# A three-round convolution and token-mixing kernel: when chunks enter their round, and where the weight loads and the adds of x are queued

## The chip, the cores and the metric

The kernel runs on one core of a Trainium2 chip. The metric is the device time of one execution in microseconds. TensorE (PE in the profile) multiplies and writes PSUM, VectorE (DVE) and ScalarE (ACT) read PSUM and work on SBUF, GpSimd (POOL) works on SBUF and issues DMAs that cast or accumulate, and SyncE (SP) issues plain DMAs.

## The reference

A short causal convolution feeds a token mixer and a channel mixer. Batch is 8, the sequence has 4224 tokens, the model width is 192.

```python
# weight: 8 heads x 7 taps, softmax over the taps; each head owns 24 channels
x = causal_conv(x, softmax(weight))          # out[s] = sum_k w[k] * x[s-6+k]
theta = x @ w_theta                          # 192 x 192
zr, zi = x * cos(theta), x * sin(theta)
y = einsum('ts,bsd->btd', w_tok_r, zr) + einsum('ts,bsd->btd', w_tok_i, zi)   # 4224 x 4224 each
u = x + y
out = u + maximum(u @ w_ch, 0)
```

The two products over tokens are nearly all of the work.

## The kernel before

**Chunks.** The tokens are cut into 33 chunks of 128. `Chunk` loads a chunk's input (`xw`, by POOL, with a halo of 16 rows that SP copies from the chunk before), and its `tasks` make the operands of the token product: `conv` (PE, evicted by ACT), `transpose` (PE; evicted by DVE for the first three chunks, by ACT afterwards), `theta` (PE, then two sines per half on ACT), `product` twice and `sums` twice (DVE). `conv` also stores the convolved x to the DRAM tensor `xs`. The second call of `sums` overwrites x, so it waits for that store.

**Units and steps.** The output tokens are cut into 17 units, 16 of them of two blocks of 128 tokens and one of a single block. A chunk must meet all 17 units. A step is one unit against all chunks that are resident; eleven chunks fit (`NW = 11`), so there are three rounds of eleven chunks. `start[k]` is the step at which chunk k enters; it stays for 17 steps. A chunk is prepared in the step before the one it enters at. There are 58 steps, and `n` is the number of chunks resident in a step. The steps from 41 on are final: they finish their unit and write the output. Of those, the steps with `n < 11` (53 to 57) are `late`.

**A step.** The complex product over two blocks is done with seven real products in place of eight (`runs`: seven runs of n chunks, two matmuls of 384 columns for each chunk). The operands of the weights are made by DVE in the step before (`w_tasks`: four transposes of 32x32 blocks, `turn`, and four sums, `wsum`), from two staging buffers `st` that POOL fills (`load_w`, four DMAs for the real weights, m = 1, and four for the imaginary ones, m = 2). There are two `st` buffers, so a load of step t+2 waits for step t+1's last transpose from the same buffer. After each run `give` adds the PSUM tile to the unit's rows `pv` on DVE; in the first round the four first writes are copies on ACT. The PSUM tiles of the runs have two buffers, so a run waits for the give of two runs before it. Rows of units that aren't finished go to DRAM (`part`) and come back 17 steps later.

**The order.** Each engine's instructions are chained by `in_order` in the order in which they are emitted. `step_events(t)` places the other work of a step by numbers from 0 to 7, the seven runs of the step. In the first steps there is no resident chunk to work on: there a loop over the eleven chunks emits the chunk's parts and, in `between`, lets the stream of the first steps advance by up to two (chunk, run) pairs at a time. `ready` holds the last chunk that is prepared, and the stream stops where it needs a later one. For the second and third chunk `between` also emits matmuls on zeros (`idle`).

**The adds of x.** u = x + y needs x once for each block. A block's x is added either by POOL in SBUF (`load_x` into `xr`, then `add_x`, which also waits for the last DVE instruction emitted before it), or in DRAM by an accumulating DMA from POOL (`add_ahead`) onto `part`. The DRAM adds are for the late steps. Each has a step of its own: 27, 29 and 31 for blocks whose x is known by then, 41 for the others.

**The end.** `outputs` finishes the final steps: cast of u to 16 bits, a transpose (by a DMA through the crossbar, `crossed`, where a step isn't late; by PE where it is), the product with `w_ch`, and `output` on DVE with the store. In the last two steps the cast of the first half of the channels is DVE's.

Of the kernel before, what the change touches and what calls it, by code (L numbers as in the profile page):

```python
# [9 lines left out]
AT = mybir.ActivationFunctionType  # L10
ALU = mybir.AluOpType
F16 = mybir.dt.float16
# [4 lines left out]
def kernel(  # L17
# [23 lines left out]
    nc = tc.nc  # L41
# [3 lines left out]
    P = nc.NUM_PARTITIONS  # L45
    assert (B, D, P) == (8, 192, 128) and S % P == 0
    N = B * D
# [4 lines left out]
    NK = S // P  # L52
# [7 lines left out]
    NU = (NT + 1) // 2  # L60
    NW = 11
    PC = 512

    base = [0, 0, 1, 1, 2, 3, 3, 4, 4, 5, 5]
    assert len(base) == NW
# [7 lines left out]
    SYNC = mybir.DependencyInfo(  # L73
        mybir.DependencyClass.Sync, mybir.DependencyReason.SCHED_ONLY
    )
    last = {}

# [31 lines left out]
    xs = dram.tile([S, N], F16, name="xs")  # L109
    part = [dram.tile([NT, P, N], F32, name=f"part{i}") for i in range(2)]  # L110
# [36 lines left out]
    def evacuate(out, in_, by_dve=False):  # L147
        if by_dve:
            dve(nc.vector.tensor_copy(out=out, in_=in_))
        else:  # L150
            act(nc.scalar.activation(out=out, in_=in_, func=AT.Copy))  # L151
# [133 lines left out]
    class Step:  # L285


        def __init__(self, t):
            self.t, self.u, self.ks = t, unit(t), active(t)
            self.n = len(self.ks)  # L290
            self.tbs = [tb for tb in (2 * self.u, 2 * self.u + 1) if tb < NT]
            self.pair = len(self.tbs) == 2
            self.first = t < NU
            self.final = t + NU >= NSTEP
            self.late = self.final and self.n < NW
            visits = [v for v in range(NU, NSTEP) if v % NU == t % NU]
            quiet = [v for v in visits if start[2 * NW - 1] < v <= 2 * NU]
            self.adds, self.ahead = [], []
            for i, tb in enumerate(self.tbs):
                known = self.known(tb)  # L300
                if t not in ([v for v in quiet if known < v - 1] or visits[-1:])[:1]:
                    continue
                if not self.late:
                    self.adds.append(i)
                else:
                    far = known <= start[2 * NW - 1]
                    self.ahead.append((i, 2 * NU - NW + 2 * (t % NU) if far else start[-1],
                                       (t // NU - 1 - far) % 2))
            self.time = 0.324 * self.n * (7 if self.pair else 4)
            self.st, self.w, self.xr, self.ub, self.uT, self.pv = {}, {}, {}, {}, {}, []  # L310

        def known(self, tb):

# [60 lines left out]
                    )  # L374
                self.pv.append(pv)

        def load_x(self, i):
            self.xr[i] = wk.tile([P, N], F16, name="xr", tag="xr", bufs=1)
            nc.sync.dma_start(
                out=self.xr[i], in_=xs[self.tbs[i] * P : (self.tbs[i] + 1) * P, :]  # L380
            )
# [9 lines left out]
        def add_ahead(self, i, which):  # L391

            tb = self.tbs[i]
# [113 lines left out]
    steps = [Step(t) for t in range(NSTEP)]  # L507
# [5 lines left out]
    def step_events(t):  # L513
        found = []
        s = steps[t]
        if t + 1 < NSTEP:
            found += steps[t + 1].w_tasks()
            found.append((1.6, steps[t + 1].load_rows))
            for i in steps[t + 1].adds:
                found.append((2 + 2 * i, lambda i=i: steps[t + 1].load_x(i)))  # L520
                found.append((3.6 + 2 * i, lambda i=i: steps[t + 1].add_x(i)))
        here = [(r, i, which) for r in steps for i, when, which in r.ahead if when == t]
        for j, (r, i, which) in enumerate(here):
            found.append((1.5 + 1.8 * j, lambda r=r, i=i, which=which: r.add_ahead(i, which)))
        if t + 2 < NSTEP:
            nxt = steps[t + 2]
            for m in (1, 2):
                found.append((1.3 + 3 * (m - 1), lambda m=m: nxt.load_w(m)))
        for at, f in outputs:
            begin = at - sum(s.time for s in steps[:t])  # L530
            if 0 <= begin < steps[t].time:
                found.append((7 * begin / steps[t].time, f))
        if t >= NU - 2:
            new = [k for k in range(NK) if start[k] == t + 2 and k >= NW]
            for k in new:
                found.append((4.5, lambda k=k: load_chunk(k)))
            at = 0.1
            for k in (k for k in range(NK) if start[k] == t + 1 and k >= NW):
                pos = [0, .5, 1.4, 2.2, 2.6, 3.1, 3.15, 3.4, 3.6]

                def add(at, j, k):
                    def go():
                        if j == 0:
                            chunks[k].todo = chunks[k].tasks()
                        next(chunks[k].todo)()
                    found.append((at, go))
                for j, p in enumerate(pos):
                    add(at + p, j, k)
                at += 2.3
        return found  # L550
# [29 lines left out]
    def idle(n):  # L580
# [17 lines left out]
        out=wsum, in_=wsb, axis=mybir.AxisListType.X, op=ALU.add  # L598
# [5 lines left out]
        out=wdiag, in0=wsb[0:KS, :, :],  # L604
        in1=ident[0:KS, 0:KS].unsqueeze(1).to_broadcast([KS, H, KS]), op=ALU.mult,
# [130 lines left out]
```

## Time and profile before

| | |
|---|---|
| median of 3 runs | 1450.12 us (1448.14 to 1450.21) |
| the profiled execution's own time | 1448.14 us |
| its span, first to last instruction | 1446.4 us |
| PE busy | 1416.3 us, 98% of the span |
| DVE busy | 979.2 us, 68% |
| POOL busy | 435.1 us, 30% |
| ACT busy | 315.5 us, 22% |
| y matmuls (`mix`, L443) | 7656, busy 1283.6 us |
| gives on DVE (L408) | 324, mean 954 ns |
| weight transposes on DVE (L336) | 224, mean 1465 ns |
| adds of x on POOL (L386) | 24, mean 3105 ns |

The profile's lines give a line of the kernel, an engine, an operation, the tiles written and read, a count, the busy time and the mean duration, and the idle time of the engine before these instructions with what ended it. A line of the windows gives a stretch of time, its length, the busy time of PE, of its weight loads (PEld), of DVE, ACT and POOL, each with a count of instructions, the granted TensorE clock as a share of full speed, the mean share of busy DMA engines, and GB/s. A line of the waits gives who waited for whom: microseconds in total, how often, the longest. A line of the timeline gives the start, the duration, the engine, the line, the operation with its tiles and the count of instructions merged.

### The profile page before, as it was taken

The page shows a single profiled execution, that of the slowest core. Times are in us where ns is not written, and L with a number is a line of the kernel's source. Part 1 is how long each engine was busy: PE and PEld are TensorE (multiplying, and loading weights), DVE is VectorE, ACT ScalarE, POOL GpSimd, SP SyncE. Part 2 cuts the span into 40 slices and gives each one's busy share as a digit, 9 for nine tenths or more (in the row PEclk, how much of TensorE's full clock was granted, in tenths as well). Part 3 has the DMA queues.
Part 4 walks back from the last instruction along what each step waited for, and adds up shares of the span by engine and source line. Part 5 has one row for each costly group of instructions (what it writes and reads, how often), then busy time and mean ns, then how long its engine had stood idle before and what let it go on. Part 6 is the DMA issues. An engine that isn't in the chain of part 4 may idle for free.

```text
span 1446.4 us, 23748 instructions
## 1 busy us (share of the span) xinstructions
PE 1416.3 (98%) x9809; PEld 887.9 (61%) x9809; DVE 979.2 (68%) x1051; ACT 315.5 (22%) x379; POOL 435.1 (30%) x655
## 2 busy tenths in 40 slices
PE   7899999999999999999999999999999999999997
PEld 5556666666666666666666666666666666666665
DVE  6893555545548777866666657877777667767686
ACT  5861101111134254000000004435210110010133
POOL 7431211111233232432433342233323123213120
PEclk9999999999999999999999999999999999999999
DMA  9986756465699998998899989999999999998893
GB/s 173 227 178 145 146 103 149 90 149 97 137 231 219 214 250 217 228 254 183 213 256 213 242 143 245 228 188 234 279 216 206 209 204 221 204 203 194 166 222 125
DMA packets 272029, 281.99 MB, mean 195 GB/s; under 512 B 106672, under 2 KB 240176, under 8 KB 271920
## 3 DMA queue, kind: packets, MB, share of 16 engines
q0 software_dynamic: 162464, 92.15, 48.4%
q1 hardware_dynamic: 71824, 178.88, 35.1%
q10 hardware_dynamic: 37632, 9.44, 4.1%
q8 instruction: 77, 1.26, 0.3%
q14 instruction: 32, 0.26, 0.1%
HBM read 245.49 MB, written 108.13 MB: 244 GB/s over the span
## 4 chain that ended last, share of the span: by engine, by line
PE 89%; DVE 4%; DMA 3%; POOL 2%; ACT 1%; issue 1%; SPq 0%; DVEq 0%; ACTq 0%; POOLq 0%
PE y L443 82%; PE v L141 5%; PE pc L210 1%; PE tp L165 1%; POOL st L323 1%; DMA xw<-in_x_dram 1%; DVE z L257 1%; DVE wt L336 1%; DVE pv L408 1%; ACT z L246 1%; DVE z L251 0%; DVE pv L476 0%; DVE wt L348 0%; POOL xw L197 0%; DMA xs<-z 0%
## 5 line engine op out<-in xcount | busy, mean ns | idle before, releaser
L443 PE MATMUL y<-z,wt 128*128 128x384 f16 x7656 | 1283.6, 326 | 10.6 <-DVE pv L408 7.5
L443 PEld LDWEIGHTS <-wt 128*128 128x128 f16 x7656 | 740.8, 98 | 488.6 <-issue 10.6
L408 DVE TENSOR_TENSOR pv<-y,pv 128x768 f32<-128x768 f32 x324 | 308.9, 954 | 323.6 <-PE y L443 282.8
L336 DVE STREAM_TRANSPOSE wt<-st 128x1408 f16<-128x1408 f16 (+7 forms) x224 | 327.8, 1465 | 48.5 <-PE y L443 39.0
L323 POOL DMA_DIRECT2D st<-in_moe_w_tok_r_dram x232 | 132.5, 578 | 466.1 <-DVE wt L336 461.0
L323 POOL DMA_DIRECT2D st<-in_moe_w_tok_i_dram x232 | 132.7, 578 | 404.4 <-DVE wt L336 388.9
L348 DVE TENSOR_TENSOR wt<-wt 128x1408 f16<-128x1408 f16 (+7 forms) x216 | 176.7, 818 | 40.8 <-PE y L443 38.4
L151 ACT ACTIVATE z<-pc 128x768 f16<-128x768 f32 x65 | 53.2, 819 | 387.2 <-PE pc L210 386.9
L151 ACT ACTIVATE ub<-pv 128x768 f16<-128x768 f32 x63 | 50.2, 835 | 333.0 <-DVE pv L408 310.4
L406 ACT ACTIVATE pv<-y 128x768 f32<-128x768 f32 x66 | 54.0, 819 | 282.0 <-PE y L443 282.0
L141 PEld LDWEIGHTS <-uT 128*128 128x128 f16 x1056 | 91.0, 98 | 25.8 <-issue 7.9
L386 POOL TENSOR_TENSOR pv<-pv,xr 128x1536 f32<-128x1536 f32 x24 | 74.5, 3105 | 68.6 <-DVE pv L476 22.1
L197 POOL DMA_DIRECT2D xw<-in_x_dram x132 | 76.4, 585 | 31.0 <-DMA xw<-xw 8.7
L476 DVE SCALAR_TENSOR_TENSOR pv<-v,pv 128x768 f32<-128x768 f32 x66 | 62.9, 954 | 27.5 <-PE v L141 27.1
L257 DVE TENSOR_TENSOR z<-z 128x768 f16<-128x768 f16 x132 | 73.4, 556 | 3.6
L151 ACT ACTIVATE uT<-tp 128x1536 f16<-128x1536 f16 (+1 forms) x48 | 58.2, 1215 | 74.4 <-PE tp L165 74.4
L246 ACT ACTIVATE z<-v,half_pi 128x768 f16<-128x768 f32 x66 | 59.8, 907 | 41.2 <-PE v L141 40.8
L251 DVE TENSOR_TENSOR z<-z 128x1536 f16<-128x1536 f16 x66 | 60.0, 947 | 7.5 <-ACT z L246 7.5
L141 PE MATMUL v<-wth,uT 128*128 128x192 f16 x528 | 55.0, 248 | 4.4 <-ACT z L246 3.0
L141 PE MATMUL v<-wch,uT 128*128 128x192 f16 x528 | 54.2, 246 | 2.1 <-DVE pv L476 1.2
L246 ACT ACTIVATE z<-v 128x768 f16<-128x768 f32 x66 | 53.4, 809 | 0.0
L210 PE MATMUL pc<-xw,bands 96*64 96x192 f16 x528 | 35.8, 258 | 2.6 <-ACT bands L625 1.1
(44 smaller groups left out, 142.4 us busy)
## 6 DMA issues: line engine op xcount, KB each, us to landing
part<-pv SPq DMA_DIRECT2D x79, 768.0 KB, 4.3
pv<-part SPq DMA_DIRECT2D x79, 768.0 KB, 6.1
out_dram<-pv SPq DMA_DIRECT2D x66, 384.0 KB, 4.3
st<-in_moe_w_tok_r_dram POOLq DMA_DIRECT2D x136, 176.0 KB, 5.5
st<-in_moe_w_tok_i_dram POOLq DMA_DIRECT2D x136, 176.0 KB, 5.1
xs<-z SPq DMA_DIRECT2D x132, 96.0 KB, 4.5
xw<-in_x_dram POOLq DMA_DIRECT2D x121, 96.0 KB, 6.1
xr<-xs SPq DMA_DIRECT2D x24, 384.0 KB, 3.7
```

What stands on the lines that cost most here:

```text
L141: pe(nc.tensor.matmul(v[:, k, b * D : (b + 1) * D], lhsT=tT[:, 3 * k + b + i, :], rhs=w[:, 2 * b + i, :], start=(i == 0), stop=(i == 1),))
L151: act(nc.scalar.activation(out=out, in_=in_, func=AT.Copy))
L197: nc.gpsimd.dma_start(out=self.xw[lo : lo + n, h, :, :], in_=x[:, t0 : t0 + n, :].rearrange("b s d -> s b d"),)
L246: act(nc.scalar.activation(**args))
L257: dve(nc.vector.tensor_tensor(out=z[:, o, :], in0=z[:, a, :], in1=z[:, b, :], op=ALU.subtract))
L323: pool(nc.gpsimd.dma_start(out=st[a * Q : (a + 1) * Q, 0:nb, :, 0:n] .rearrange("i r bt s -> i (r bt) s"), in_=w[self.tbs[0] * P : (self.t ...
L336: dve(nc.vector.transpose(self.w[name][:, 0 : self.n, :, :], self.st[int(name[1])][:, int(name[0]) - 1, :, 0 : self.n * Q] .rearrange("p b ...
L348: dve(nc.vector.tensor_tensor(out=self.w[name][:, 0 : self.n, :, :], in0=self.w[a][:, 0 : self.n, :, :], in1=self.w[b][:, 0 : self.n, :, : ...
L386: ins = pool(nc.gpsimd.tensor_tensor(out=self.pv[i], in0=self.pv[i], in1=self.xr[i], op=ALU.add))
L408: dve(nc.vector.tensor_tensor(out=o, in0=yv, in1=o, op=ALU.add))
L443: pe(nc.tensor.matmul(y[cn][:, q, 0:BH], lhsT=self.w[wn][:, c, :, :].rearrange("p bt i -> p (bt i)"), rhs=chunks[k].z[:, zn, q * BH : (q + ...
L476: dve(nc.vector.scalar_tensor_tensor(out=ub, in0=channel_mix(self.uT[i][:, 6 * g : 6 * g + 6, :], wch), scalar=0.0, in1=ub, op0=ALU.max, o ...
```

## The change

- **Entry.** The three rounds get lists of their own. The first round's chunks enter at steps 0, 0, 0, 1, 1, 2, 2, 3, 3, 4, 4 in place of 0, 0, 1, 1, 2, 3, 3, 4, 4, 5, 5. The second round's enter two at a time at steps 18 to 22 and one at 23. The third round's list is as before. The number of chunks in steps 0 to 5 is 3, 5, 7, 9, 11, 11 in place of 2, 4, 5, 7, 9, 11; in steps 17 to 22 it is 8, 8, 8, 8, 8, 10 in place of 9, 9, 10, 9, 9, 9; in steps 35 to 40 it is 9, 9, 9, 8, 8, 9 in place of 9, 9, 10, 9, 9, 9. There are 58 steps as before.
- **Start-up.** x of chunk 2 is loaded ahead of the weights of step 0, and x of chunk 3 ahead of the weights of step 1. DVE's weight work of step 0 is emitted after the sums of chunk 0, not after the theta of chunk 0.
- **Adds of x.** On POOL: x is loaded at the add, at 3.3 and 5.0 of the step, and the add doesn't wait for DVE any more. In DRAM: the adds of a late step come four steps ahead of it, in steps 49 to 53.
- **Casts.** All casts are ACT's.

```diff
-    base = [0, 0, 1, 1, 2, 3, 3, 4, 4, 5, 5]
-    start = [base[k % NW] + (NU + 1) * (k // NW) for k in range(NK)]
+    base = [[0, 0, 0, 1, 1, 2, 2, 3, 3, 4, 4],
+            [0, 0, 1, 1, 2, 2, 3, 3, 4, 4, 5],
+            [0, 0, 1, 1, 2, 3, 3, 4, 4, 5, 5]]
+    start = [base[k // NW][k % NW] + (NU + 1) * (k // NW) for k in range(NK)]
...
+            self.ahead = self.late or 0 <= t + NU - NSTEP < 2
...
-        def load_x(self, i):
-            self.xr[i] = wk.tile([P, N], F16, name="xr", tag="xr", bufs=1)
-            nc.sync.dma_start(
-                out=self.xr[i], in_=xs[self.tbs[i] * P : (self.tbs[i] + 1) * P, :]
-            )
...
-            ins = pool(nc.gpsimd.tensor_tensor(
-                out=self.pv[i], in0=self.pv[i], in1=self.xr[i], op=ALU.add
-            ))
-            tc.add_manual_dep(ins.ins, last["dve"].ins.name, SYNC, reason="pace")
...
+            rows = slice(self.tbs[i] * P, (self.tbs[i] + 1) * P)
+            if not self.ahead:
+                xr = wk.tile([P, N], F16, name="xr", tag="xr", bufs=1)
+                nc.sync.dma_start(out=xr, in_=xs[rows, :])
+                pool(nc.gpsimd.tensor_tensor(
+                    out=self.pv[i], in0=self.pv[i], in1=xr, op=ALU.add
+                ))
+                return
             for cols in (slice(0, HN), slice(HN, N)):
                 pool(nc.gpsimd.dma_start(
-                    out=part[which][tb, :, cols], in_=xs[tb * P : (tb + 1) * P, cols],
-                    accum_op=ALU.add,
+                    out=part[(self.t // NU - 1) % 2][self.tbs[i], :, cols],
+                    in_=xs[rows, cols], accum_op=ALU.add,
                 ))
...
-            evacuate(self.ub[i][:, cols], self.pv[i][:, cols], self.t >= NSTEP - 2 and g == 0)
+            act(nc.scalar.activation(
+                out=self.ub[i][:, cols], in_=self.pv[i][:, cols], func=AT.Copy
+            ))
...
-            for i in steps[t + 1].adds:
-                found.append((2 + 2 * i, lambda i=i: steps[t + 1].load_x(i)))
-                found.append((3.6 + 2 * i, lambda i=i: steps[t + 1].add_x(i)))
+            if not steps[t + 1].ahead:
+                for i in steps[t + 1].adds:
+                    found.append((3.3 + 1.7 * i, lambda i=i: steps[t + 1].add_x(i)))
+        for s in steps[t:]:
+            if s.ahead and t == s.t - (4 if s.late else 10):
+                for i in s.adds:
+                    found.append((3.3 + 1.7 * i, lambda s=s, i=i: s.add_x(i)))
...
     steps[0].load_rows()
+    load_chunk(2)
     for m in (1, 2):
         steps[0].load_w(m)
-    load_chunk(2)
+    load_chunk(3)
     for m in (1, 2):
         steps[1].load_w(m)
...
-        if i == 1:
-            for _, f in steps[0].w_tasks():
-                f()
         if i + 3 < NW:
             load_chunk(i + 3)
...
         if old:
             old.sums(1)
+        if i == 1:
+            for _, f in steps[0].w_tasks():
+                f()
         between(1)
```

More of the change, by code (lines that the diff above doesn't have):

```diff
@@ L62 @@
     PC = 512
-    base = [0, 0, 1, 1, 2, 3, 3, 4, 4, 5, 5]
-    assert len(base) == NW
-    start = [base[k % NW] + (NU + 1) * (k // NW) for k in range(NK)]
+    base = [[0, 0, 0, 1, 1, 2, 2, 3, 3, 4, 4],
+            [0, 0, 1, 1, 2, 2, 3, 3, 4, 4, 5],
+            [0, 0, 1, 1, 2, 3, 3, 4, 4, 5, 5]]
+    assert all(len(b) == NW for b in base)
+    start = [base[k // NW][k % NW] + (NU + 1) * (k // NW) for k in range(NK)]
     NSTEP = start[-1] + NU
@@ L71 @@
         mybir.DependencyClass.NoSync, mybir.DependencyReason.DATA
-    )
-    SYNC = mybir.DependencyInfo(
-        mybir.DependencyClass.Sync, mybir.DependencyReason.SCHED_ONLY
     )
@@ L295, in __init__ @@
             self.late = self.final and self.n < NW
+            self.ahead = self.late or 0 <= t + NU - NSTEP < 2
             visits = [v for v in range(NU, NSTEP) if v % NU == t % NU]
-            quiet = [v for v in visits if start[2 * NW - 1] < v <= 2 * NU]
-            self.adds, self.ahead = [], []
+            self.adds = []
             for i, tb in enumerate(self.tbs):
[L300 to L303, printed above, removed]
+                at = [v for v in visits if self.known(tb) < v - 1 and v + NU < NSTEP
+                      and start[2 * NW - 1] < v <= 2 * NU]
+                at = at[0] if at else visits[-1]
+                if t == at:
                     self.adds.append(i)
[L305 to L308, printed above, removed]
             self.time = 0.324 * self.n * (7 if self.pair else 4)
-            self.st, self.w, self.xr, self.ub, self.uT, self.pv = {}, {}, {}, {}, {}, []
+            self.st, self.w, self.ub, self.uT, self.pv = {}, {}, {}, {}, []
         def known(self, tb):
@@ L375, in load_rows @@
                 self.pv.append(pv)
-        def load_x(self, i):
-            self.xr[i] = wk.tile([P, N], F16, name="xr", tag="xr", bufs=1)
-            nc.sync.dma_start(
-                out=self.xr[i], in_=xs[self.tbs[i] * P : (self.tbs[i] + 1) * P, :]
-            )
-        def add_x(self, i):
-            ins = pool(nc.gpsimd.tensor_tensor(
-                out=self.pv[i], in0=self.pv[i], in1=self.xr[i], op=ALU.add
-            ))
-            tc.add_manual_dep(ins.ins, last["dve"].ins.name, SYNC, reason="pace")
-        def add_ahead(self, i, which):
-            tb = self.tbs[i]
+        def add_x(self, i):
+            rows = slice(self.tbs[i] * P, (self.tbs[i] + 1) * P)
[6 more added lines that the diff above has]
+                return
             for cols in (slice(0, HN), slice(HN, N)):
                 pool(nc.gpsimd.dma_start(
-                    out=part[which][tb, :, cols], in_=xs[tb * P : (tb + 1) * P, cols],
-                    accum_op=ALU.add,
+                    out=part[(self.t // NU - 1) % 2][self.tbs[i], :, cols],
+                    in_=xs[rows, cols], accum_op=ALU.add,
                 ))
@@ L518, in step_events @@
             found.append((1.6, steps[t + 1].load_rows))
-            for i in steps[t + 1].adds:
-                found.append((2 + 2 * i, lambda i=i: steps[t + 1].load_x(i)))
-                found.append((3.6 + 2 * i, lambda i=i: steps[t + 1].add_x(i)))
-        here = [(r, i, which) for r in steps for i, when, which in r.ahead if when == t]
-        for j, (r, i, which) in enumerate(here):
-            found.append((1.5 + 1.8 * j, lambda r=r, i=i, which=which: r.add_ahead(i, which)))
+            if not steps[t + 1].ahead:
[5 more added lines that the diff above has]
+                    found.append((3.3 + 1.7 * i, lambda s=s, i=i: s.add_x(i)))
         if t + 2 < NSTEP:
```

## The prediction

> **What bounds the kernel now.** The page comes first: is one engine full all the way?
>
> ```profile
> span 1446.4 us, 23748 instructions
> ...
> PE 1416.3 (98%) x9809; PEld 887.9 (61%) x9809; DVE 979.2 (68%) x1051; ACT 315.5 (22%) x379; POOL 435.1 (30%) x655
> ...
> L443 PE MATMUL y<-z,wt 128*128 128x384 f16 x7656 | 1283.6, 326 | 10.6 <-DVE pv L408 7.5
> ```
>
> PE is the bound and idles 30 us. The count of y matmuls doesn't change (each of 33 chunks meets every unit once), nor does the number of steps (58). So only PE's idle time can change, and the waits of PE, with the windows, say where it lies (PE busy, PEld, DVE, ACT, POOL in each):
>
> ```profile
> PE y L443 <- DVE pv L408: 5.1, 5, 2.5
> PE y L443 <- ACT pv L406: 3.0, 3, 1.2
> ...
> PE pc L210 <- DMA xw<-in_x_dram: 0.9, 1, 0.9
> ```
>
> ```profile
> 90.00:100.00 10.00, 10.00 (x71) 6.55 (x70) 9.76 (x15) 6.24 (x9) 2.34 (x4) 1.00 0.84 241
> 100.00:110.00 10.00, 7.54 (x48) 4.33 (x46) 9.79 (x12) 0.63 (x1) 3.40 (x6) 1.00 0.59 78
> ...
> 140.00:440.00 300.00, 300.00 (x1898) 181.73 (x1896) 155.33 (x140) 46.18 (x56) 61.92 (x108) 1.00 0.66 136
> ```
>
> These waits are those of the first 110 us. From 110 to 1340 us PE waits 2.9 us in all, and 3.6 us at the end. The start-up alone has slack, and it ends when DVE, full from 90 us on, gives PE a PSUM buffer back: the last wait, 2.46 us, ends at 104.61. DVE's timeline shows how the start-up is ordered:
>
> ```profile
> 24.68 0.70 DVE L336 STREAM_TRANSPOSE wt<-st 128x512 f16<-128x512 f16 x1
> 25.59 0.96 DVE L149 COPY uT<-tp 128x1536 f16<-128x1536 f16 x1 [0.20 <-PE tp L165]
> ...
> 46.24 1.15 DVE L257 TENSOR_TENSOR z<-z 128x768 f16<-128x768 f16 x2
> ```
>
> The first weight transpose of step 1 comes just ahead of the copy that releases chunk 2's theta matmuls. Today its weights landed long ago; the reader should keep this pair in mind.
>
> **Start-up.** Three edits meet: step 0 takes three chunks, step 0's weight work moves behind chunk 0's sums, and x of chunks 2 and 3 is issued ahead of weights. What they remove: the 0.9 us wait for chunk 3's x, and some waits at runs of two chunks, which last 0.65 us against 0.8 to 0.95 us for one eviction.
> What they add, in order. DVE ran step 0's weight work at 15.35 to 18.1, in a gap waiting for PE; now the gap stays empty and the work starts when chunk 0's sums end, at 24.77. Four transposes and four sums at three chunks lie between the rows at two (0.43, 0.29) and four (0.70, 0.42): 4 x 0.57 + 4 x 0.36 = 3.7, so to 28.5. Step 1's first weight buffer is free after the second transpose, 25.9; POOL issues four loads by 28.5 (4 x 0.57); they land between 2.4 and 5 us later, 3.5 taken: 32.0. DVE waits for them, 3.5 us. Then the transpose (0.84) and the copy of chunk 2: 33.8, against 26.55 today. PE stands from about 27.1 to 33.8, since its queue is in order. Behind those loads on POOL stand x of chunks 4 and 5 (issued 30.8 to 35.4, landing 4.9 later, so 38 for chunk 4, whose matmuls come at about 39: covered by 1 us, 2 us lost if they are late). On SP chunk 2's copies between buffers now come ahead of chunk 0's stores of x (14.48 today, about 15.5 then), which chunk 0's last two sums await at 23.5; at 4.6 to land, 3 us of cover stay. Step 0's own weights are issued 2.3 later, behind x of chunk 2, and aren't used before 24.77.
> Part of the delay is absorbed: today PE loses 3.1 us at 33 to 39 to evictions of step 0, which come later now. DVE: chunk 1 products and sums (1.82 + 2.34) to 37.95, chunk 2 to 42.1, a transpose to 43.0; chunk 3's sine I put at 44.6 (45.0 today), then product 0.91, sum 0.48, transpose 0.84, product 0.91: chunk 3's sums start at 47.8, today at 46.24.
> From there to the give that frees PE, DVE's queue as built holds: seven chunks at 4.16 and chunk 3's sums 2.34, 31.5; eight gives at 0.95, 7.6; transposes 0.84 + 4 x 1.10 + 4 x 1.37, 10.7; weight sums 3 x 0.48 + 4 x 0.63 + 3 x 0.79, 6.3. Together 56.1. Today the same list is 54.9 in 58.4 us (46.24 to 104.61), so 3.5 idle. Half of that idle: 47.8 + 56.1 + 1.6 = 105.5.
> At its stall PE has done 224 y matmuls today and 196 then, 28 fewer, each 0.1625 us (1938 in 315.1 us): 4.55 us more left. 105.5 + 4.55 - 104.6 = **+5.4**. Loads landing at 30.9 and no idle give +2.8; 33.5, all the idle and late x give +9.
>
> *The clock.* In the windows of 2 us the granted clock is 0.72 at 38:40, 0.50 at 40:42, 0.93 at 42:44, after PE's gaps at 33 to 39. I let one such dip move to 34 us and count nothing.
> The Trainium skill ("TensorE: Matmul & The Clock Gate", Part 1) says that an idle window of about 3.4 us halves the clock and about as long a busy one restores it, which speaks against a PE gap of 6.7 us. If its dip came in addition to today's, the sum would be 2 us more by an estimate from that page.
>
> **Later rounds.** Steps 17 to 21 now have eight chunks and two new ones each. DVE per step: seven gives 6.7, four transposes (between 1.10 and 1.37) 4.9, four sums 2.8, two chunks 8.3: 22.7. PE: 8 x 14 x 0.1625 = 18.2, and two chunks at 3.5 (0.52 x 2 + 0.83 + 0.82 x 2): 25.2. That is 90%, against 23.5 of 27.5 in today's two-chunk steps at nine (85%), where waits of 0.3 to 0.7 us appear. Five such steps in a row, a little each: +0.8 (-0.5, if fewer single collisions fall badly, to +4, if each step loses one eviction, 0.95).
>
> **Adds of x on POOL** lose their wait on a DVE instruction, and x is loaded at the add. POOL may wait a landing more (3.7) ahead of a weight load. Today DVE waits 8.1 us for weights, and PE for none of it: DVE waits 283 us for PE, which is the cover. 0 (-0.5 to +1). Without cover an add costs its 3.1.
>
> **Late adds in DRAM.** 18 accumulating DMAs that ran at 678 to 1046 us now run in steps 49 to 53, beside the crossbar transposes, two ahead of each weight load of POOL. Each takes 0.86 to issue and 9.1 to land. A load issued at 4.3 of 7 of a step is used at 2.2 of the next: 4.9/7 of 25 us, 17 us, against 1.7 + 9.1 + 5.9. Little is left over, so +0.3 (0 to +3); their absence from 678 to 1046 frees nothing that PE waits for.
>
> **Last casts.** Three casts of 0.55 on DVE become 0.83 on ACT. ACT's last part is on the path: a 0.83 cast started at 1434.05 delays the copy at 1434.66 by 0.2, and the first is 0.28 longer: +0.5 (0 to 1.3).
>
> Sum: 5.4 + 0.8 + 0 + 0.3 + 0.5 = +7.0. The profiled execution took 1448.14 (span 1446.4 and 1.7 around it), 2.0 below the median of 1450.12. 1446.4 + 7.0 + 1.7 = 1455.1, and 1457 against the median.
>
> **Rivals.** *Faster:* the start-up follows PE's and ACT's cadence, not DVE's queue. Then the last theta matmul (93.2 today) comes 1.3 earlier for eight y matmuls fewer ahead of it, and up to 4.6 (PE's idle time from 40 to 93, evictions above all) earlier still: 87.3 to 91.9; the give follows 7.6 later as today, 94.9 to 99.5. With 4.55 for the 28 matmuls that is -5.2 to -0.6, about -3: 1447. For it speak the 8.1 us of eviction waits; against it DVE's 98% in the same place. It decides only if chunk 3's sums start before 104.6 - 4.55 - 56.1 = 43.9.
> *No change:* DVE's idle time today (3.5, and 3.5 at the wait for loads) hides it all: within 2.9 us, 1450.
> *More than start-up:* the two-chunk steps lose an eviction each (+4), and the late adds hold one weight load past its use (+3): 5.4 + 4 + 3 + 0.5 = +13, 1463. For it: DMA share about 1.0 in those stages. Against it: PE full in all of them now.
>
> **Numbers.** A measurement can tell 0.2%, 2.9 us. Forecast, +3 to +10: 0.62; the third rival: 0.13; no change 0.12; faster 0.13. Slower is 0.75. The range runs from 1449, most of no change, to 1463, the third rival's sum.
>
> **What would show it.** A DVE wait for the r weights of step 1 at about 28 us; chunk 2's copy at 33 to 35; a PE gap there with the clock falling; PE's last start-up wait ending at 103 to 108 with 196 y matmuls done; PE waits of under 0.7 in steps 17 to 21; the last casts on ACT. It is wrong if that last wait ends before 100, or if PE loses more than 4 us after 110.

## The result, and the profile after

The changed kernel takes 1484.92 us (median of 4 runs, 1478.22 to 1490.04), the kernel before, measured beside it, 1449.13. The ratio is 1.0246, interval 1.0203 to 1.029: slower by about 36 us where +7 was forecast and 1463 was the upper end. The sign was right, and the size was wrong by a factor of five.

The profiled execution of the changed kernel is its slowest, 1490.04 us with a span of 1488.2. From its page, the span, the engines and the y matmuls:

```profile
span 1488.2 us, 23738 instructions
...
PE 1426.6 (96%) x9809; PEld 890.9 (60%) x9809; DVE 1016.4 (68%) x1048; ACT 318.1 (21%) x382; POOL 435.9 (29%) x655
...
L431 PE MATMUL y<-z,wt 128*128 128x384 f16 x7656 | 1289.1, 327 | 17.1 <-DVE pv L396 12.9
```

The work of PE is the same, 9809 matmuls. The span is 41.8 us longer: PE stands idle for 61.6 us in place of 30.1 (31.5 more), and is busy for 10.3 us more on the same matmuls; the granted clock is lower after its gaps (0.91 over the first 112 us in place of 0.98, 0.94 from 1340 us to the end of the run). DVE, with fewer instructions, is busy for 37 us more. The waits of PE name the places (total, how often, the longest):

```profile
PE v L140 <- DMA uT<-ub: 13.7, 3, 7.5
PE y L431 <- DVE pv L396: 12.9, 16, 2.8
PE pc L209 <- ACT z L150: 6.0, 1, 6.0
PE v L140 <- DVE uT L148: 5.0, 2, 4.8
...
PE y L431 <- DVE wt L331: 2.5, 1, 2.5
```

Of these five, only the second is in the profile before (7.5, 10, 2.5). The windows put them in time (columns as in the table of before: PE, PEld, DVE, ACT, POOL, then clock, DMA share and GB/s):

```profile
90.00:100.00 10.00, 9.84 (x90) 6.77 (x89) 7.67 (x10) 9.14 (x12) 2.34 (x4) 0.96 0.39 67
100.00:110.00 10.00, 8.52 (x59) 5.17 (x57) 9.69 (x14) 4.35 (x6) 0.00 (x0) 1.00 0.37 70
110.00:120.00 10.00, 7.55 (x47) 4.57 (x47) 8.02 (x10) 1.62 (x2) 5.69 (x10) 1.00 0.90 189
140.00:440.00 300.00, 300.00 (x1848) 180.64 (x1847) 146.28 (x128) 38.94 (x48) 59.56 (x104) 1.00 0.61 124
440.00:600.00 160.00, 155.89 (x1226) 99.09 (x1224) 122.58 (x153) 68.72 (x78) 49.38 (x87) 1.00 1.00 232
1340.00:1400.00 60.00, 53.75 (x343) 33.51 (x341) 34.93 (x39) 6.31 (x8) 21.51 (x29) 0.94 1.25 189
```

Before, PE lost 2.9 us in all between 110 and 1340. Now it loses 4.1 us between 440 and 600 alone, where the kernel before has

```profile
440.00:600.00 160.00, 159.27 (x1206) 100.93 (x1204) 126.47 (x148) 57.43 (x66) 52.59 (x86) 1.00 0.99 230
```

It loses 2.4 us between 600 and 870, where it lost nothing before, and 6.2 between 1340 and 1400. So the start is not the only stage that loses time.

DVE's timeline shows the pair that the prediction pointed at, the weight transpose of step 1 ahead of chunk 2's copy:

```profile
26.42 0.36 DVE L343 TENSOR_TENSOR wt<-wt 128x384 f16<-128x384 f16 x1
30.48 0.85 DVE L331 STREAM_TRANSPOSE wt<-st 128x640 f16<-128x640 f16 x1 [3.69 <-DMA st<-in_moe_w_tok_r_dram]
31.24 0.92 DVE L148 COPY uT<-tp 128x1536 f16<-128x1536 f16 x1
```

The wait is there, 3.69 us (3.5 was worked out), and the copy is 5.65 us later than before. But 50 us later comes a wait that no sentence of the prediction mentions. ACT's timeline and then PE's:

```profile
84.73 0.81 ACT L150 ACTIVATE z<-pc 128x768 f16<-128x768 f32 x1 [7.71 <-DMA part<-pv]
```

```profile
85.59 0.85 PE L209 MATMUL pc<-xw,bands 96*64 96x192 f16 x8 [5.96 <-ACT z L150]
...
112.45 5.85 PE L431 MATMUL y<-z,wt 128*128 128x384 f16 x35 [2.78 <-DVE pv L396]
```

ACT wants to write chunk 9's z tile and waits until a store to `part` has landed: the tile takes a buffer of the z pool that a row of step 1 still occupies (`z_free` below tests this). SP issues that store at 78.55 us, and it lands 6.08 us later:

```profile
78.55 0.34 SPq L444 DMA_DIRECT2D part<-pv  x1
```

In the kernel before, step 1's two rows go out about 8 us earlier. They land after 3.4 and 4.8 us, by 75.6, one to three microseconds ahead of the first copy into chunk 9's z tile:

```profile
70.14 1.02 SPq L456 DMA_DIRECT2D part<-pv  x2
```

```profile
76.74 0.93 ACT L151 ACTIVATE z<-pc 128x768 f16<-128x768 f32 x1
```

PE, which waits for ACT, stands for 6 us, DVE runs dry (7.15 us), and the last wait of the start ends at 112.45, not at 105.5. At that moment 196 y matmuls have been done, as predicted.

### The profile page after: what moved, and what is told of

It is laid out like the page before. It is cut to its first block, busy times and chain, and to the rows that moved or that the text cites. A ratio compares the mean times of both kernels' runs of the same rounds, so it can differ in the third digit from the quotient of the medians.

```text
span 1488.2 us, 23738 instructions
## 1 busy us (share of the span) xinstructions
PE 1426.6 (96%) x9809; PEld 890.9 (60%) x9809; DVE 1016.4 (68%) x1048; ACT 318.1 (21%) x382; POOL 435.9 (29%) x655
## 4 chain that ended last, share of the span: by engine, by line
PE 76%; DVE 11%; DMA 7%; ACT 2%; issue 2%; SPq 1%; POOL 0%; ACTq 0%; DVEq 0%
PE y L431 70%; PE v L140 4%; DMA uT<-ub 3%; DVE pv L396 2%; DVE wt L343 2%; DVE z L250 2%; DVE z L256 2%; DVE wt L331 2%; ACT z L245 1%; PE tp L164 1%; PE pc L209 1%; DMA xw<-xw 1%; DMA st<-in_moe_w_tok_r_dram 1%; DMA part<-pv 1%; DMA xs<-z 1%
## 5 line engine op out<-in xcount | busy, mean ns | idle before, releaser
L431 PE MATMUL y<-z,wt 128*128 128x384 f16 x7656 | 1289.1, 327 | 17.1 <-DVE pv L396 12.9
L431 PEld LDWEIGHTS <-wt 128*128 128x128 f16 x7656 | 742.4, 98 | 498.7 <-issue 22.6
L331 DVE STREAM_TRANSPOSE wt<-st 128x1408 f16<-128x1408 f16 (+8 forms) x224 | 327.5, 1465 | 46.9 <-PE y L431 41.5
L343 DVE TENSOR_TENSOR wt<-wt 128x1408 f16<-128x1408 f16 (+8 forms) x216 | 217.0, 1005 | 46.8 <-PE y L431 44.6
L378 POOL TENSOR_TENSOR pv<-pv,xr 128x1536 f32<-128x1536 f32 x24 | 74.9, 3120 | 15.1 <-DMA xr<-xs 11.1
L140 PE MATMUL v<-wch,uT 128*128 128x192 f16 x528 | 55.5, 249 | 15.6 <-DMA uT<-ub 13.7
```

Source lines behind the costliest of these rows:

```text
L140: pe(nc.tensor.matmul(v[:, k, b * D : (b + 1) * D], lhsT=tT[:, 3 * k + b + i, :], rhs=w[:, 2 * b + i, :], start=(i == 0), stop=(i == 1),))
L331: dve(nc.vector.transpose(self.w[name][:, 0 : self.n, :, :], self.st[int(name[1])][:, int(name[0]) - 1, :, 0 : self.n * Q] .rearrange("p b ...
L343: dve(nc.vector.tensor_tensor(out=self.w[name][:, 0 : self.n, :, :], in0=self.w[a][:, 0 : self.n, :, :], in1=self.w[b][:, 0 : self.n, :, : ...
L378: pool(nc.gpsimd.tensor_tensor(out=self.pv[i], in0=self.pv[i], in1=xr, op=ALU.add))
L431: pe(nc.tensor.matmul(y[cn][:, q, 0:BH], lhsT=self.w[wn][:, c, :, :].rearrange("p bt i -> p (bt i)"), rhs=chunks[k].z[:, zn, q * BH : (q + ...
```

## The experiments

The change consists of four edits that can be made one by one: the start (entry lists, order of the first loads, place of step 0's weight work), the POOL adds, the late DRAM adds, and the casts. My first theory after the trace was a sum over places: start 12, two-chunk steps and POOL adds 7.7, the end 22.

### The edits alone

`late_alone`, the late DRAM adds alone:

```
-  self.ahead.append((i, 2 * NU - NW + 2 * (t % NU) if far else start[-1],
-                     (t // NU - 1 - far) % 2))
+  self.ahead.append((i, t - 4, (t // NU - 1) % 2))
...
-  found.append((1.5 + 1.8 * j, ... add_ahead(i, which)))
+  found.append((3.3 + 1.7 * j, ... add_ahead(i, which)))
```

> The kernel before with one edit alone: the 18 accumulating DMAs of the last nine blocks are issued four steps ahead of their step (steps 49 to 53) and no longer in steps 27 to 41. Theory (they hold the crossbar transposes back): uT<-ub lands in 10 to 27 us instead of 5 to 9, PE waits 10 to 15 us for uT behind those transposes between 1330 and 1410, two or three halvings of the granted clock follow, and the time is 17 to 25 us above before. Rival 1 (the transposes suffer only because the other edits shift the end's timing or put all casts on ACT): 0 to +5. Rival 2, the prediction's own reading (a weight load is held a little): +0.3, at most +3.

Measured: 1449.03, ratio 1.0001 (0.9991 to 1.001). No cost at all; the theory fell, as did my reading of the end as an effect of this edit by itself. The transposes do land later (median 9.1 us of those after 1200, longest 10.9, in place of 6.9 and 8.3), but nobody waits.

`start_alone`, the three edits of the start:

> The kernel before with the new entry lists, the new order of the first loads and step 0's weight work behind chunk 0's sums; adds and casts as before. Theory: the start-up costs 12 us (10 us of PE idle time and about 2 of halved clock, the wait of 6 for a z tile that a row of step 1 still holds among them) and the two-chunk steps 3 to 5: +15 to +17. Rival (the prediction's sum: start-up 5.4, later rounds 0.8, the wait for the z tile being an accident of that run): +6. Rival 2 (the start-up's loss is made good later): under +4.

Measured: 1471.56, ratio 1.0163 (1.0147 to 1.0179), +22.6. This is the largest part by far. The wait for the z tile is there again (6.0), so it is no accident of one run, and the last stall ends at 113.34.

`pool_alone`, the POOL adds alone:

```
-  found.append((2 + 2 * i, ... load_x(i)))
-  found.append((3.6 + 2 * i, ... add_x(i)))
+  found.append((3.3 + 1.7 * i, ... load_x(i)))
+  found.append((3.3 + 1.7 * i, ... add_x(i)))
...
-  tc.add_manual_dep(ins.ins, last["dve"].ins.name, SYNC, reason="pace")
```

> The kernel before with the 24 adds of x on POOL changed alone: x loaded at the add, no wait on a DVE instruction. Theory: the adds now lie beside weight sums of DVE, which hold each other up: weight sums of the steps with adds take up to 4 us, DVE is busy 25 to 40 us more in all, PE waits 2 to 4 us more between 600 and 870 and about as much after 1050 none: +2 to +4. Rival (the prediction): DVE's waits for PE cover it, 0 (-0.5 to +1). What it leaves to see is whether the DVE growth comes with this edit alone.

Measured: 1451.40, ratio 1.002 (1.0011 to 1.003), +2.4. The group of DVE's weight sums, from the page of before and from this run's:

```profile
L348 DVE TENSOR_TENSOR wt<-wt 128x1408 f16<-128x1408 f16 (+7 forms) x216 | 176.7, 818 | 40.8 <-PE y L443 38.4
...
L348 DVE TENSOR_TENSOR wt<-wt 128x1408 f16<-128x1408 f16 (+7 forms) x216 | 211.2, 978 | 40.7 <-PE y L442 38.2
```

One of these sums on DVE's timeline, and what POOL does at that time:

```profile
703.07 4.49 DVE L348 TENSOR_TENSOR wt<-wt 128x1408 f16<-128x1408 f16 x1
```

```profile
703.69 3.12 POOL L386 TENSOR_TENSOR pv<-pv,xr 128x1536 f32<-128x1536 f32 x1
```

A sum of this shape takes 0.88 us with POOL idle. Beside the add it takes 4.49, and the add takes its usual 3.12. PE then waits for DVE's give (1.5 us between 600 and 870, nothing before). In the profile before, one add between 600 and 1340 us runs beside a weight sum (3.42 us at 612.70); in this run more than half of them do. The removed wait let an add begin only after a DVE instruction, but the edit also moves the adds, from 3.6 and 5.6 of the step, behind the sums emitted at 3.05, 3.3 and 5.1, to 3.3 and 5.0. Which of the two brings adds and sums together isn't shown.

`after_adds_back`, the changed kernel with only the late DRAM adds put back into steps 27 to 41:

> The changed kernel with the accumulating DMAs of the last nine blocks put back into steps 27 to 41. Theory: the end of the run recovers, PE waits for uT<-ub vanish, 17 to 25 us below the changed kernel, so +14 to +22 against before. Rival (the end's loss comes from the shifted start or from the casts on ACT): within 5 us of the changed kernel, +30 to +36.

Measured: 1473.82, ratio to before 1.0179 (1.016 to 1.0197), 11.1 below the changed kernel. Between the two theories. The sum of the start and the POOL adds alone is 25.0 and this kernel is 24.9 above before, so the casts on ACT, the one other edit in it, are worth nothing that these runs can tell (each interval reaches about 2.5 us to either side, and 0.5 was forecast). The late DRAM adds are worth 0 alone and 11 in company.

### Which company

`late_pool` and `late_start` join the late DRAM adds to one other edit each.

> The kernel before with two edits: the late accumulating DMAs (alone: 1.0001 of before) and the POOL adds of x (alone: 1.002). Question: with which other edit do the late DMAs cost the 11 us that putting them back gave in the changed kernel. Theory I: the adds of x now stand on POOL right ahead of the DRAM adds of steps 51 and 52, so these are issued 3 us later, at the moment the two crossbar transposes go out: +8 to +19 against before, PE waits for uT<-ub of 5 to 15 us after 1320. Theory II (it takes the shifted start, or the casts on ACT): +2.4, no wait for uT.

Measured: 1455.55 (1453.64 to 1462.61), ratio 1.0061 (1.0036 to 1.0085): 6.7 us above before, 4.2 above the POOL adds alone. The runs lie 9 us apart, and the profiled one is the slowest, 1462.61. That is less than the 11.1 that the late adds cost in the changed kernel.

> The kernel before with the late accumulating DMAs and the edits of the start (alone: +22.6). Theory I (POOL's adds are the partner): +22 to +23, no PE wait for uT<-ub. Theory II (the shifted start and the later chunks are the partner): +28 to +38 with such waits at the end.

Measured: 1470.93, ratio 1.0157 (1.0141 to 1.0174), the same as the start alone, and no wait for uT. So, of the two, the partner is the POOL adds. The two timelines at the same step, first `late_alone`, then `late_pool` (POOL's DRAM adds and ACT's transposes, picked from all engines):

```profile
1319.20 1.76 POOL L394 DMA_DIRECT2D part<-xs  x2
1324.38 1.70 ACTq L158 DMA_TRANSPOSE uT<-ub  x1
1327.95 5.45 ACTq L158 DMA_TRANSPOSE uT<-ub  x1
```

```profile
1328.89 1.76 POOL L393 DMA_DIRECT2D part<-xs  x2
1329.30 2.19 ACTq L158 DMA_TRANSPOSE uT<-ub  x1
1333.20 8.69 ACTq L158 DMA_TRANSPOSE uT<-ub  x1
```

Alone, the DRAM adds are issued 5.2 us ahead of the first transpose. With the other edit the add of x stands ahead of them on POOL (3.1 us), and they go out 0.4 us ahead of it. The queue of the transposes in the 35 us around that moment (its packets, megabytes, and share of 16 DMA engines), again `late_alone` and then `late_pool`:

```profile
q10 hardware_dynamic: 3136, 0.79, 13.6%
```

```profile
q10 hardware_dynamic: 3136, 0.79, 44.8%
```

The same packets occupy the DMA engines 3.3 times as long. One transpose lands after 21.8 us, PE waits 5.5 us, and the clock halves for 6.8 us. The changed kernel has it at two pairs of transposes, with up to 26.6 us to land, 13.7 us of waits, and 17 us at half clock after 1380. What is shown is that it takes both edits. That the moment of issue does it is a reading of the traces. The same share over 35 us, from 9 us ahead of a pair of transposes, is 10.3 to 19.5% for the pairs after 1240 us in kernels without DRAM adds there. It is 13.4 to 18.2% for the twelve pairs in `late_alone`, `late_start`, `late_pool` and the changed kernel whose DRAM adds go out 5.2 to 5.5 us ahead, and 44.8 and 28.2% for the two pairs with 0.4 us. But the changed kernel's last pair has DRAM adds 5.0 and 3.7 us ahead of it and still 33.5%, so the distance alone doesn't explain that one. The version with the two lines of POOL's queue swapped, which would test the reading, has no measurement.

### The start

`z_free` takes away what the z tile waits for:

```
-  if not self.final:
-      for i, tb in enumerate(self.tbs):
-          nc.sync.dma_start(out=part[(self.t // NU) % 2][tb, :, :], in_=self.pv[i])
+  if not self.final and self.t != 1:
+      for r in ([steps[1], self] if self.t == 2 else [self]):
+          for i, tb in enumerate(r.tbs):
+              nc.sync.dma_start(out=part[(self.t // NU) % 2][tb, :, :], in_=self.pv[i])
```

> The start edits alone (1471.6), but step 1's two rows are not stored at the end of step 1: their places in DRAM are written from step 2's rows at the end of step 2 (so the output of these blocks is that of other data), and the z buffers that the rows hold come free with the last give. Theory (chunk 9's first copy waits 6 us for the row's store to land, and this stops every engine at 80 to 87 us): the wait goes, the last stall of the start ends at 105 to 107 instead of 113.3, one or two halvings of the clock go, and the time falls by 7 to 11, to +12 to +16 against before. Rival (DVE's queue sets the last stall anyway, and DVE would fill the time with other waits): the wait goes but the time falls by less than 3.

Measured: 1463.41, ratio 1.0111 (1.0094 to 1.0128), 8.1 below `start_alone`. ACT's line for chunk 9's z tile, and PE's last stall of the start:

```profile
80.46 0.81 ACT L153 ACTIVATE z<-pc 128x768 f16<-128x768 f32 x1 [1.59 <-DVE pv L410]
```

```profile
106.70 3.60 PE L445 MATMUL y<-z,wt 128*128 128x384 f16 x13 [2.79 <-DVE pv L410]
```

The tile now waits 1.59 us for a give, not 7.7 for a landing, and the stall ends 6.6 us earlier than in `start_alone`. The theory holds: this one wait is about 8 of the start's 22.6.

`lists_alone` keeps only the entry lists:

> The kernel before with the three entry lists alone: step 0's weight work stays in DVE's early gap and the first loads stay in their order. Theory: the wait at chunk 2's copy (3.6) and the 2.5 for the first weight go, a wait for chunk 2's or 3's x of 1 to 2 comes back, while the wait of 6 for the z tile of chunk 9 and the 4.8 of the two-chunk steps stay: +12 to +17. Rival 1 (the order of the first loads and the weight work behind chunk 0's sums make most of the start's loss): under +8. Rival 2 (they repay part of what the lists cost): over +22.

Measured: 1462.58, ratio 1.0099 (1.0082 to 1.0116), +13.7; z wait (5.9) and two-chunk waits as in `start_alone`. So the lists cost 13.7, and the two other edits of the start 9.0 on top.

### The start again, without crossbar transposes

For the further runs the transposes of steps 41 to 52 are PE's, in all kernels alike; the start isn't touched by that.

> The kernel before with the 24 crossbar transposes of steps 41 to 52 made by PE instead (12 transposes of 128x128 for each block and two evictions on ACT). It is the base of the runs with nx in their name. Estimate from the rows of before: 288 transposes of 0.082 us (108 took 8.8 us) on a PE that is full there, 23.6 us, so about 1472; the start is untouched.

Measured: 1466.25, ratio to before 1.0118 (1.0101 to 1.0135). The estimate of 23.6 was too high because a transpose in this place costs less than one at the run's end: PE is busy for 17.6 us more, 0.061 for each.

> The changed kernel with the same replacement. Theory (the late accumulating DMAs cost their 11 us only through the crossbar transposes): against nx_before the change now costs what start and POOL adds cost together, +23 to +26, and PE has no wait above 2.5 us after 1050. Rival (accumulating DMAs at the end hold up other traffic too, weight loads and row loads): +30 to +37, with waits of PE or DVE for st or pv at the end.

Measured: 1493.53, 27.3 above nx_before, and no wait of PE above 1.1 us after 1050. That is 2.3 more than the start and POOL adds cost beside crossbar transposes (25.0). By `nx_start` below, the start costs only 19.2 in these kernels, which with the POOL adds' 2.4 leaves 5.7, and the late adds may be part of that. The trace has 2.1 us of it as PE waits for ACT's casts (at 1100.81 and 1218.05), and no wait of PE or DVE for a DMA after 1050. So the long waits at the end need the crossbar transposes; that the late adds cost nothing without them isn't shown.

`nx_order`: order of the loads and place of the weight work, old lists.

> nx_before with the new order of the first loads and step 0's weight work behind chunk 0's sums, entry lists as before. With the lists in place these two are worth 1471.6 - 1462.6 = 9. Theory (the weight work in front of step 1's loads makes DVE wait, whatever the lists are): chunk 2's copy comes at 31 to 33 instead of 25.6, +5 to +9 against nx_before. Rival (only three chunks in step 0 make it late, and DVE's idle time takes it up): under +3.

Measured: 1469.62, 3.4 above nx_before, between theory and rival. Chunk 2's copy comes at 30.94 (25.37 in nx_before), as the theory has it, yet PE's last stall ends only 1.5 us later (108.44 against 106.90). With two chunks in step 0 the idle time of DVE does take up most.

`nx_lists_first`: the new list in the first round only.

> nx_before with the new entry list in the first round only; the second and third round keep the list of before, and the order of the first loads stays. All lists cost +13.7 without the replacement. Theory (the five two-chunk steps of the second round cost 3.4 us at 440 to 600 and 1.4 at 870 to 1050): +8 to +10 against nx_before, PE waits of 0.7 and about 2 in these windows as before, and the wait of 6 for chunk 9's z tile stays. Rival (a later stage gives the second round's loss back): +12 to +15.

Measured: 1481.90, 15.7 above nx_before: the rival's number, for a reason that neither had. The window of 440 to 600:

```profile
440.00:600.00 160.00, 151.14 (x1192) 96.25 (x1191) 122.69 (x154) 68.66 (x78) 47.74 (x84) 1.00 1.00 237
```

PE idles 8.9 us there, where all lists together lose 4.1 and the old ones 0.7. The first round's chunks leave early because they entered early; with the second round's old entries, steps 20 and 21 are left with seven chunks and prepare two each. What costs is few chunks in a step that prepares new ones; the second list softens what the first does. The experiment did not isolate what I meant it to.

`nx_start`, all edits of the start:

> nx_before with all edits of the start (entry lists, order of the first loads, step 0's weight work behind chunk 0's sums): the base of the next two. With crossbar transposes these cost 22.6. All theories: +21 to +24 against nx_before (1466.3), so 1487 to 1490.

Measured: 1485.43, 19.2 above nx_before, less than the +21 to +24 expected; the runs don't say why (the kernel before, measured beside each of the two, differs by 0.4).

`nx_warm` fills PE's gap with matmuls on zeros:

```
   v = banks("v")
+  for _ in range(warm):          # 14 for the first theta of chunk 2, else 0
+      pe(nc.tensor.matmul(v[:, 0, 0:BH], lhsT=noise[:, 0:P], rhs=noise, start=True, stop=True))
```

> nx_start with 14 matmuls on zeros ahead of chunk 2's first theta matmuls, into the bank that these overwrite, where PE stands still for 3.6 us. They do no work of the kernel and only keep PE busy. Theory (part of the start's loss is the clock halved after PE's gaps): one or two of the halvings between 36 and 50 us go, 2 to 4 us below nx_start. Rival 1 (DVE's queue and the wait for chunk 9's z tile set the start's end, so PE's clock there does not matter, as the prediction counted): within 1 us of nx_start. Rival 2 (the added matmuls delay the rest): 1 us or more above.

Measured: 1484.09, 1.3 below nx_start, and the runs of the two overlap (1483.69 to 1485.38 against 1484.84 to 1486.09). In the profiled runs the clock is at half for 6.8, 3.4 and 6.8 us in nx_start (from 31.0, 41.3 and 85.7 us) and for 3.4, 3.4 and 10.2 us in nx_warm (from 25.0, 42.1 and 83.0): 17.1 us in both. The last stall ends at 115.04 against 114.62, no earlier. The zeros moved the halvings and didn't shorten them in all, so the run doesn't price the clock in the start, and neither the theory nor the first rival is decided by it.

`nx_start_wold` puts step 0's weight work back into DVE's early gap:

> nx_start with step 0's weight work back in DVE's early gap; the lists and the order of the first loads stay changed. Theory (the place of the weight work delays step 1's loads and so chunk 2's copy, the prediction's first term): DVE has no wait for st at 28, chunk 2's copy at 25 to 27, 7 to 9 us below nx_start. Rival (the order of the loads, weights behind x of chunks 2 and 3, is what is late): within 3 of nx_start, with a DVE wait for st at step 0's own weights.

Measured: 1480.61, 4.8 below nx_start. DVE's timeline has the pair without a wait, at 26 in place of 32 us:

```profile
26.12 0.84 DVE L334 STREAM_TRANSPOSE wt<-st 128x640 f16<-128x640 f16 x1
26.88 0.92 DVE L151 COPY uT<-tp 128x1536 f16<-128x1536 f16 x1
```

The copy moved as the theory said, the time by less than it said: the last stall ends 5.8 us earlier (108.85 against 114.62).

`nx_lists`, the lists alone, tells what the order of the loads costs beside that:

> nx_before with the three entry lists alone. With crossbar transposes they cost 13.7; nx_start_wold, with the new order of loads besides, is 14.4 above nx_before. Theory (the order of the loads is worth little): +12 to +15 against nx_before. Rival (the lists cost more and the earlier x gives some back): +16 or more; rival 2 (the order of the loads costs part of the 14.4): under +11.

Measured: 1479.69, 13.4 above nx_before: nx_start_wold, with the new order of loads, is 0.9 above it. The order of the loads is worth nothing that these runs can tell, and the place of the weight work, 4.8, is most of the 5.7 that the two edits cost here.

### All of it undone

`nx_three_undone` has the lists, the order of loads, the late DRAM adds and the casts of the change, without the other causes.

> nx_after with three of its causes undone at once: step 0's weight work back in DVE's early gap, the POOL adds of x as before, and step 1's two rows not stored at step 1's end (their places in DRAM are written from step 2's rows, so these blocks hold other data). The entry lists, the order of the first loads, the late accumulating DMAs and the casts on ACT stay changed. Theory (the causes add up): what is left is the two-chunk steps' 4.8 and the start's last stall at about 102 with 28 y matmuls fewer (4.55), against 104.6 to 106.9 in the kernels with the old lists: +5 to +8 against nx_before (1466.3), so 1471 to 1474. Rival (another wait takes the place of those undone): +11 or more.

Measured: 1472.63, 6.4 above nx_before, the theory's number: nothing new takes the place of what was undone. It is 20.9 below nx_after, where the three edits taken one by one are worth 15.3 (8.1, 2.4 and 4.8). Each difference is uncertain by about 3.5 us, so these runs can't tell whether the 5.6 between is noise or what the edits cost together. The place differs a little from what was expected: PE's last stall of the start ends at 99.32, and up to 130 us PE idles as long as in nx_before (18.9 us against 19.1). The start is free again, and the two-chunk steps have 4.6 of the rest (idle 4.1 and 3.5 us in their two windows against 0.9 and 2.1).

## Why the prediction was wrong, step by step

| part | forecast | measured | from |
|---|---|---|---|
| start-up, without the z tile's wait | +5.4 | +6.6 | stall of z_free: 106.70 + 4.55 - 104.61 |
| wait for chunk 9's z tile | not seen | +8.1 | start_alone less z_free |
| two-chunk steps | +0.8 (to +4) | +4.8 | windows 440:600 and 870:1050 |
| adds of x on POOL | 0 (to +1) | +2.4 | pool_alone |
| late DRAM adds | +0.3 (to +3) | 0 alone, +11 in the change | late_alone, after_adds_back |
| casts | +0.5 | not told from 0 | after_adds_back less the sum |

The measured column adds up to 33 of the 36. The 3 are missing in the start: z_free is 14.5 above before, and its stall and the two-chunk steps make 11.4. For this I have only a part: the profiles of start_alone and z_free show one more halving of the clock behind the last stall (3.4 us long, 1.7 lost), the changed kernel's doesn't.

**Start-up, the part that was seen.** Weights of step 1 awaited (3.69 for 3.5; POOL's four loads were put to end at 28.5, which the terms given there make 28.2), copy of chunk 2 done at 32.16 (33.8: the weight work began at 23.21, 1.6 us earlier than I put it), chunk 3's sums at 47.95 (47.8), 196 y matmuls at the stall. The 47.95 is right by the term for chunk 3's sine, not by the late copy: DVE waits 1.31 and 2.44 us for sines in between. With the z wait away the stall ends at 106.70; 105.5 was worked out. That fits a start whose end DVE's queue sets. The faster rival is refuted by its own condition: chunk 3's sums did not start before 43.9.

**Start-up, the step that failed.** The working listed DVE's queue to its end and put half a known idle time into it. It never asked whether each engine would have its buffers. The z pool has 11 buffers for 16 tiles of the start: 11 chunks, four rows of steps 0 and 1, and the zeros. The last chunks take the buffers of step 1's rows, once these are stored. Step 0 and 1 are now 56 (chunk, run) pairs long in place of 42, so the rows are stored later, while chunk 9's conv comes at its old time. The profile before had the numbers for it: the two rows go out from 70.14 us on, have landed by 73.5 and 75.6, and chunk 9's copy starts at 76.74, a cover of one to three microseconds. In the changed kernel the store goes out at 78.55, and ACT, idle from 77.0, starts the copy at 84.73.

**Two-chunk steps.** The arithmetic (90% full, a little lost in each) was right in kind, and the size was wrong: 0.8 was put for the five steps, and PE's idle time between 440 and 600 grew by 3.4. Each step loses one wait for an eviction, as the third rival had it at 0.95: PE's timeline of the changed kernel between 440 and 600 has

```profile
475.22 0.48 PE L431 MATMUL y<-z,wt 128*128 128x384 f16 x2 [0.53 <-DVE pv L396]
...
500.64 0.48 PE L431 MATMUL y<-z,wt 128*128 128x384 f16 x2 [0.54 <-DVE pv L396]
...
577.55 0.48 PE L431 MATMUL y<-z,wt 128*128 128x384 f16 x2 [1.20 <-DVE pv L396]
```

and two more of 0.53; under 0.7 was forecast. I counted only the second round's entry; the steps where the third round enters (35 to 40) lost 1.4 more, since the second round leaves earlier too.

**Adds on POOL.** The cover was named (DVE waits 283 us for PE) and the price of losing it too (3.1), but the edit was costed as a wait removed. What it left out is that an add lengthens a DVE sum that runs beside it: the sum above became 3.6 us longer beside an add of 3.1. The Trainium skill states this (page "SBUF — State Buffer", section "Who interferes with whom"): a VectorE instruction with two inputs in SBUF contends with a GpSimd instruction that reads SBUF. The trace agrees with it, 0.88 us becoming 4.49. The prediction did not weigh it. Whether the wait or the place of the adds had kept the two apart is open.

**Late DRAM adds.** The step asked who is queued behind them on POOL (the weight loads, rightly harmless) and not whom they meet in the DMA engines. The front of the same step names the crossbar transposes and drops them. The single edit turned out free; it costs 11 in the change, and 4 with the POOL adds alone. That another edit's 3.1 us of POOL time makes the price is the likely reading, not shown.

**The clock.** It was counted as nothing, and the first step, that only PE's idle time can change, doesn't hold: PE's busy time is 10.3 of the 41.8 us by which the profiled span grew. Before, the clock is at half once in the start, for 3.4 us; in the changed kernel for 6.8, 3.4 and 6.8 us there, and for 17 us after 1380. How much of it the start's end feels stays open.

**The rivals.** "More than start-up" had the right mechanism for the two-chunk steps (+4), and the wrong one for the late adds. My criterion for being wrong, PE losing more than 4 us after 110, is met.

## What to carry to other kernels

When work at the start grows, follow the buffers as well as the queues: list the tiles that share a pool, and for each late one ask whose store or last reader it waits for. A wait that costs nothing may be keeping two instructions apart; ask what overlaps when it is gone or when its instruction moves. Edits to one engine's queue don't add up when their DMAs meet: cost them together, by the time of issue that the built order gives.

## What the runs showed of the hardware that I had not expected

- A DVE sum of two SBUF tiles took 4.49 us beside a POOL add (0.88 without), although its record begins 0.6 us before the add's. That add isn't slowed (3.12 us); over the 24 adds the mean is 3.162, and 3.105 before. A give, which reads PSUM and one SBUF tile, keeps its 0.96 us beside a POOL add.
- Accumulating DMAs beside crossbar transposes: harmless in the twelve pairs where they were issued 5.2 to 5.5 us ahead (13.4 to 18.2% of the DMA engines' time for 3136 transpose packets), slow in the two where they were issued 0.4 us ahead (44.8% in late_pool, 28.2% in the changed kernel) and in the pair behind the second of these (33.5%). The cost differs from run to run: these two kernels spread over 9 and 12 us, after_adds_back over 4.
